# Decays by running products, and fewer raw weights held, in a fused retention and two-expert kernel

## Chip, cores, metric

The kernel runs on one core of a Trainium2 chip. The metric is the device time of one launch, in microseconds (us), as the median of several runs. Engines: TensorE (PE in the profile, its weight loads PEld), VectorE (DVE), ScalarE (ACT), GpSimd (POOL), and SyncE (SP), whose queue issues nearly all DMAs.

## What is computed

A retention layer (linear attention with a decay for each head) over two sequences of 768 positions, 8 heads of 64, in blocks of 64; then two experts, 512 to 2048 to 512 (squared ReLU) and 512 to 1536 to 512 (sigmoid gate), on the 1536 rows.

```python
# for each block of 64 positions
intra = (q_b @ k_b.T) * Dmask            # Dmask[i, j] = lam ** (i - j) for i >= j, else 0
out_b = intra @ v_b + (q_b * lam ** (i + 1)) @ state
state = lam ** 64 * state + (k_b * lam ** (63 - i)).T @ v_b
...
x = retention output as (1536, 512)
g = relu(x @ w_in) ** 2
x = g @ w_out
x = (sigmoid(x @ w_gate) * (x @ w_val)) @ moe2_w_out
```

## The kernel before, in words

Data are float32. A product of float32 matrices is made as three products of rounded halves (hi, lo): a hi part is a cast on ScalarE (`whi`, `xh`, `gh`, `ah`, `xch`), a lo part a subtraction on VectorE (`wlo`, `xl`, `gl`, `al`, `xcl`).

The weights come as raw words of 8 bytes. `load_w` brings one raw tile of 512 KB into a buffer of the pool `wp`, `scale_words` turns it with two ScalarE operations (lines 153 and 158) into two halves, and `join_words` puts these together with a shift and an add on VectorE (lines 164 and 169). Two weights go together as a couple: `couple_act`, `couple_dve`, `couple_split` are the ScalarE part, the VectorE part and the hi and lo split. Each whole weight is also stored to DRAM (`w32`) for later stages, 4 us of planner time after its add. Weights of the second expert are converted one at a time (`conv_act`, `conv_dve`) in the stage after the first Strassen stage.

The order on each engine is the order of the program text; a planner clock (`clock`, moved by `passed`, matmuls at 0.2267 us) only places the entries of an agenda (`at(pos, fn)`), such as splits of x, loads and stores. Nothing in the program text waits by hand: an operation waits for its operands and for the earlier users of the buffer that it gets. The pool `wp` has 27 buffers of 4 KB per partition, shared by q/k and k/v tiles, raw weights, couples, the split blocks of x and the weights of the Strassen stages; `up` has 27 of half that size.

Stages in time:

1. The lead: decays (`powers`, `decay_rows`, `decay_table`), loads, attention of the first two pairs of chunks (`PAIRS`, `LEAD`), with filler matmuls between (`warm_up`). Decays are powers: POOL computes W = lam ** ex; ScalarE's queue stores it to `w_dram`; SP loads the table D from there with a shifted row for each partition; 16 products on PE spread W into the rows L. For a pair: `att_scores`, `att_mask` (scores times D), `keys_of` and `query` (decayed k and q, on GpSimd), `att_uv`, `state_a` and `state_b` (states), `att_out`, `settle`, `att_past`, `att_x` (output split into x0).
2. A loop of 16 steps (`step_1`) for the first expert on the first 512 rows: 12 matmuls of `stage_a` (line 576) and 12 of `stage_b` of the step before (line 590), with the attention of the other four pairs between them (`SLOTS`, `LOADS`). `combine_x` splits the sums of the other rows' x blocks during the last steps.
3. `strassen` for the first expert's input product on the other 1024 rows: 8 units of 7 blocks of 6 matmuls (line 790), in the order B11, T4 of the unit before, T1, T2, B22, T3, B21. Weights of the next unit are split meanwhile (`load_a`, `combine_a`, `high_a`, `low_a`).
4. `pair_out` (line 1181), the first expert's output product, with the conversion of the second expert's weights.
5. The same for the second expert (`step_2`, `strassen` with 12 units, `blocks_out`).

## Time and profile before

| | |
|---|---|
| median of 3 runs | 626.39 us (625.79 to 628.44) |
| the profiled execution | 627.19 us |
| its span, first to last instruction | 625.3 us |
| PE busy | 584.6 us (93%) |
| VectorE / ScalarE / GpSimd busy | 452.3 / 340.5 / 59.9 us |
| mean granted TensorE clock | 0.984 of full speed |

Times in rows are from the start of the span. Busy PE includes matmuls in flight, so a stage's matmul count says more than its busy share.

### The profile page before, as it was taken

How to read it: one execution, taken by the hardware profiler on the slowest of the kernel's cores; microseconds unless marked ns; L12 is line 12 of the kernel's file. 1: busy time of each engine (PE TensorE's matmuls, PEld its weight loads, DVE VectorE, ACT ScalarE, POOL GpSimd, SP SyncE). 2: the span in 40 equal slices, each digit the busy share in tenths (PEclk: the TensorE clock that was granted, in tenths of full speed). 3: DMA queues.
4: the chain of work that ended last, by engine and by line, in shares of the span. 5: the costliest groups of instructions: out<-in, count | busy, mean ns of one | idle time of the engine just before them, and what ended most of it. 6: DMA issues, size and time to landing. Idle time of an engine off the chain costs nothing.

```text
span 625.3 us, 10317 instructions
## 1 busy us (share of the span) xinstructions
PE 584.6 (93%) x3924; PEld 471.7 (75%) x3924; DVE 452.3 (72%) x640; ACT 340.5 (54%) x538; POOL 59.9 (10%) x54
## 2 busy tenths in 40 slices
PE   7679998997888789999999999999999999999997
PEld 6657877865666667788888888888887888878885
DVE  2559978679657666766774688787477886779975
ACT  2267664597533453767664766454445634476561
POOL 4341354000000000000000000011011011000000
PEclk9869999998989999999999999999999999999999
DMA  8957995673214432999999699988544878397581
GB/s 304 396 212 281 332 305 187 220 246 134 68 68 124 163 116 88 304 368 415 412 409 380 226 338 286 349 281 248 133 116 102 239 213 210 133 363 291 180 329 67
DMA packets 69475, 150.63 MB, mean 241 GB/s; under 512 B 7089, under 2 KB 15281, under 8 KB 69426
## 3 DMA queue, kind: packets, MB, share of 16 engines
q1 hardware_dynamic: 65184, 144.08, 64.7%
q0 software_dynamic: 3360, 3.93, 4.2%
q10 hardware_dynamic: 882, 1.97, 1.0%
q8 instruction: 30, 0.49, 0.3%
q14 instruction: 19, 0.16, 0.1%
HBM read 106.17 MB, written 42.21 MB: 237 GB/s over the span
## 4 chain that ended last, share of the span: by engine, by line
PE 71%; DVE 11%; ACT 8%; DMA 5%; issue 4%; SPq 0%; DVEq 0%; ACTq 0%
PE p L790 20%; PE p L576 15%; PE p L1181 14%; PE p L590 10%; PE p L1110 7%; DMA qk<-in_qk 3%; PE p L477 2%; DVE c L804 2%; DVE al L769 2%; DMA gr<-gs 2%; ACT ah L763 2%; DVE wlo L228 1%; ACT s L799 1%; ACT whi L225 1%; DVE gq L977 1%
## 5 line engine op out<-in xcount | busy, mean ns | idle before, releaser
L790 PE MATMUL p<-xch,ah 128*128 128x512 f32 x280 | 112.2, 401 | 14.6 <-DVE c L804 10.3
L790 PE MATMUL p<-xch,al 128*128 128x512 f32 x280 | 109.9, 392 | 0.0
L790 PE MATMUL p<-xcl,ah 128*128 128x512 f32 x280 | 109.6, 391 | 0.0
L790 PEld LDWEIGHTS p<-xch,ah 128*128 128x128 f32 x280 | 52.9, 189 | 34.2 <-DVE c L804 13.6
L790 PEld LDWEIGHTS p<-xch,al 128*128 128x128 f32 x280 | 52.9, 189 | 11.4
L790 PEld LDWEIGHTS p<-xcl,ah 128*128 128x128 f32 x280 | 53.0, 189 | 10.4
L1110 PE MATMUL p<-gq,wq 128*128 128x512 f32 x252 | 57.9, 390 | 1.0 <-DVE wq L1067 1.0
L799 ACT COPY s<-p 128x512 f32<-128x512 f32 x60 | 34.8, 587 | 40.5 <-PE p L790 40.3
L1110 PEld LDWEIGHTS p<-gq,wq 128*128 128x128 f32 x252 | 47.1, 188 | 11.7 <-DVE wq L1067 1.6
L169 DVE CUSTOM_DVE_ANT_0 j<-j,r 128x1024 uint16<-128x1024 uint16 (+1 forms) x52 | 47.8, 920 | 4.5 <-ACT r L158 0.5
L153 ACT ACTIVATE j<-raw 128x512 f32<-128x512 f32 x68 | 45.5, 669 | 8.3 <-DMA raw<-in_w 6.7
L1181 PE MATMUL p<-g2l,whi 128*128 128x512 f32 x128 | 49.8, 389 | 0.0
L1181 PE MATMUL p<-g2h,wlo 128*128 128x512 f32 x128 | 49.8, 389 | 0.0
L1181 PE MATMUL p<-g2h,whi 128*128 128x512 f32 x128 | 49.8, 389 | 0.0
L804 DVE TENSOR_TENSOR c<-p,s 128x512 f32<-128x512 f32 x60 | 40.5, 685 | 12.4 <-PE p L790 12.4
L576 PE MATMUL p<-xh,whi 128*128 128x512 f32 x160 | 45.1, 405 | 1.2 <-ACT xh L539 1.2
L158 ACT ACTIVATE r<-raw 128x512 int32<-128x512 uint32 x68 | 45.2, 665 | 1.4 <-PE p L576 1.4
L625 ACT CAST gh<-g 128x512 fp32r<-128x512 f32 x28 | 17.4, 620 | 49.3 <-DVE g L617 25.5
L576 PE MATMUL p<-xh,wlo 128*128 128x512 f32 x160 | 43.7, 395 | 0.0
L576 PE MATMUL p<-xl,whi 128*128 128x512 f32 x160 | 43.6, 395 | 0.0
L738 POOL DMA_DIRECT2D as<-w x6 | 5.6, 933 | 382.7 <-DMA as<-w 355.8
L627 DVE TENSOR_TENSOR gl<-g,gh 128x512 fp32r<-128x512 f32 x28 | 21.0, 748 | 26.7 <-ACT gh L625 26.7
(140 smaller groups left out, 1087.8 us busy)
## 6 DMA issues: line engine op xcount, KB each, us to landing
raw<-in_w SPq DMA_DIRECT2D x68, 512.0 KB, 7.1
w<-j SPq DMA_DIRECT2D x68, 256.0 KB, 4.9
u<-w SPq DMA_DIRECT2D x52, 256.0 KB, 5.1
a<-w SPq DMA_DIRECT2D x20, 512.0 KB, 4.1
g<-g SPq DMA_DIRECT2D x32, 256.0 KB, 4.2
g<-g SPq DMA_DIRECT2D x16, 512.0 KB, 8.0
kv<-in_kv SPq DMA_DIRECT2D x12, 512.0 KB, 7.6
gr<-gs SPq DMA_DIRECT2D x24, 256.0 KB, 5.7
```

The lines of the kernel that those rows point to most:

```text
L153: nc.scalar.activation(j, t[:, :, 1].bitcast(F32), AF.Prelu, scale=2.0**-80 if flip else 2.0**-112, alpha=2.0**-32 if flip else 2.0**32,)
L158: nc.scalar.activation(r, low, AF.Copy, scale=2.0**-29)
L169: nc.vector.tensor_tensor(out=j, in0=j, in1=r, op=ALU.add)
L576: nc.tensor.matmul(acc, lhsT=a[:, kk * P : (kk + 1) * P], rhs=b[:, kk, :], start=i == 0, stop=i == 11,)
L590: nc.tensor.matmul(acc[e], lhsT=a[:, e * P : (e + 1) * P], rhs=b, start=first and i == 0, stop=last and i == 2,)
L625: nc.scalar.copy(gh, src)
L627: lambda: nc.vector.tensor_tensor(out=gl, in0=src, in1=gh, op=ALU.subtract)
L790: nc.tensor.matmul(acc, lhsT=w[:, col, kk * P : (kk + 1) * P], rhs=x[:, kk, :], start=start and i == 0, stop=stop and i == 5, skip_group_c ...
L799: nc.scalar.copy(s, acc)
L804: nc.vector.tensor_tensor(out=c, in0=acc, in1=s, op=ALU.add)
L1110: nc.tensor.matmul(acc[k], lhsT=a[:, wn], rhs=block_of(b, gn), start=first and n == 0, stop=last and n == 3 * len(group) - 1,)
L1181: nc.tensor.matmul(acc[e, t], lhsT=a[:, e * P : (e + 1) * P], rhs=b[:, t, :], start=first and i == 0, stop=last and i == 2,)
```

## The change

Decays become running products. A table of steps (lam, with 0 at the head of each row) and a table of spots (1 where a product starts) are made, and two scans on VectorE multiply along: one gives D, one gives the rows L; W is lam times the last column of D. The power, the stores to `w_dram`, the loads of D and the 16 products on PE are gone. All lead loads but q6 go through SP in one line. The order of the lead is another: the first pair is masked at once and put out before the second pair's scores; the first two weights are converted one by one and not as a couple; the fillers are 40, 12, 30 and 8 matmuls; `settle` is on ScalarE for the two lead pairs; v2 and v8 are loaded later. `couple_act` loads only weights of the first expert, and three raw weights of the second are loaded 14 us of planner time before `pair_out`. In `step_1`, `couple_act` stands at the end. The square in odd steps is on ScalarE as in even ones. Stores of whole weights come 7 us after their add and not 4. B21 is split last but two, and the places of the x sums are shifted.

```diff
-FILL = (16, 24, 44)
+FILL = (40, 12, 30, 8)
...
-    couples = [((1, 0, 0), (1, 1, 0))]
+    couples = [((1, 0, 0),), ((1, 1, 0),)]
...
-            at(clock[0] + 4.0, stored)
+            at(clock[0] + 7.0, stored)
...
         if more:
-            load_w(2)
+            load_w(sum(key[0] == 1 for key in to_load[: len(keys)]))
...
+        shift = unit("shift", I32)
+        nc.gpsimd.iota(shift, pattern=[[0, H], [1, SUB]], base=0, channel_multiplier=1)
...
+        nc.vector.memset(by_seq(step_d)[:, :, :, 0:1], 0.0)
+        nc.scalar.copy(seen, warm[:, 0:1])
...
         nc.vector.tensor_scalar(
+            out=spot_d, in0=shift, scalar1=float(2 * SUB - 1), scalar2=None, op0=ALU.is_equal
         )
...
         nc.vector.scalar_tensor_tensor(
+            out=spot_d, in0=shift, scalar=float(SUB - 1), in1=spot_d,
+            op0=ALU.is_equal, op1=ALU.add,
         )
...
+        nc.vector.memset(by_seq(step_l)[:, :, :, 0:1], 0.0)
+        nc.vector.memset(spot_l, 0.0)
+        nc.vector.memset(by_seq(spot_l)[:, :, :, 0:1], 1.0)
+        lam_r = pairs_of(lam8)
+        nc.vector.tensor_copy(by_seq(step_d)[:, :, :, 1:], lam_r.to_broadcast([P, 2, 4, SUB - 1]))
+        nc.gpsimd.tensor_copy(lam_half[half(0)], lam_r[half(0)])
+        for s in range(2):
+            nc.gpsimd.tensor_copy(lam_half[half(1), s], lam_r[half(1), 1 - s])
+        nc.gpsimd.tensor_copy(by_seq(step_l)[:, :, :, 1:], lam_half.to_broadcast([P, 2, 4, SUB - 1]))
+
+        def scan(out, step, spot):
+            nc.vector.tensor_tensor_scan(
+                out=out, data0=step, data1=spot, initial=0.0, op0=ALU.mult, op1=ALU.add
+            )
+
+        scan(flat(D), step_d, spot_d)
+        nc.vector.tensor_tensor(
+            out=pairs_of(W), in0=lam_r, in1=decay[:, :, :, SUB - 1 :], op=ALU.mult
         )
+        scan(flat(rows), step_l, spot_l)
+        nc.vector.tensor_tensor(out=G, in0=lam_half, in1=L[:, :, :, SUB - 1 :], op=ALU.mult)
...
-        nc.vector.tensor_copy(seen, o_t[pair][1][:, 1, 3, SUB - 1 :])
+        copy = nc.scalar.copy if pair[0] < LEAD else nc.vector.tensor_copy
+        copy(seen, o_t[pair][1][:, 1, 3, SUB - 1 :])
...
-        if ph == 1 and f % 2:
-            nc.scalar.activation(r, acc[0], AF.Relu)
-            nc.vector.scalar_tensor_tensor(
-                out=g, in0=acc[0], scalar=0.0, in1=r, op0=ALU.max, op1=ALU.mult
-            )
-        elif ph == 1:
+        if ph == 1:
...
-            lambda: split_x("B21", b21),
...
             lambda: split_x("T3", t["T3"]),
+            lambda: split_x("B21", b21),
...
         attend(2 * f)()
-        couple_act()
...
         last()
+        couple_act()
...
-        powers()
-        load("q0 q7 v0 v6 w v1")
-        decay_table()
-        load("q1 q8", nc.scalar)
-        load("v7 w w w")
+        load("q6", nc.scalar)
+        decays()
+        load("q0 q7 v0 v6 w q1 q8 v1 v7 w w w q2 q9")
         warm_up(WARM)
...
-        decay_rows()
...
-        keys_of(0)
-        keys_of(6, nc.vector)
-        query(6)
-        query(0)
-        query(7)
         att_scores(first)
         warm_up(FILL[0])
+        keys_of(0)
+        query(0)
+        query(6)
+        run(att_mask(first))
+        keys_of(6, nc.vector)
         att_uv(first)
         warm_up(FILL[1])
+        query(7)
+        couple_act()
         state_a(first)
-        state_b(first)
         keys_of(1)
+        mid = decayed(st_t[first][1])
         query(1)
+        att_out(first)
+        settle(first)
+        run(couple_dve())
+        plus(S[2], uv_t.pop(first)[1], mid)
+        att_scores(second)
+        att_past(first)
+        warm_up(FILL[2])
+        tt[0] = decayed(S[2], nc.gpsimd)
         keys_of(7)
         query(8)
-        att_scores(second)
-        warm_up(FILL[2])
-        run(att_mask(first) + att_mask(second))
+        run(att_mask(second))
+        x = att_x(first)
+        lo = couple_split()
+        run(x)
+        run(lo)
         couple_act()
-        load("q2 q9")
-        att_out(first)
-        settle(first)
         att_uv(second)
-        att_past(first)
-        x = att_x(first)
+        state_a(second)
+        load("v2 v8")
+        att_out(second)
+        settle(second)
+        warm_up(FILL[3])
+        att_past(second)
+        x = att_x(second)
         run(couple_dve())
         run(x)
         lo = couple_split()
-        state_a(second)
-        att_out(second)
-        settle(second)
-        att_past(second)
-        x = att_x(second)
-        run(lo + x)
+        run(lo)
         couple_act()
         state_b(second)
...
-        combine_x(1, [T1 + d for d in (-25, -23, -21, -18.5, -16, -13, -10.5, -7, -4, 1, 4)])
+        combine_x(1, [T1 + d for d in (-25, -22, -19.5, -17, -14, -10, -7, -4, -1, 2, 4)])
...
+        for k in range(3):
+            at(T2 - 14.0 + k, lambda: load_w(1))
```

## Rows read from the trace of the kernel before

**Rows 1.** Busy time by stage: stretch, length, each engine's busy us (instructions), PEclk, DMA share, GB/s.

```profile
0.00:37.39 37.39, 24.41 (x641) 22.18 (x641) 13.68 (x24) 8.38 (x14) 11.76 (x16) 0.90 0.93 351
37.39:50.20 12.81, 11.77 (x40) 8.59 (x43) 9.80 (x11) 10.06 (x17) 7.37 (x5) 0.77 0.27 88
50.20:122.28 72.08, 70.12 (x1196) 56.21 (x1196) 61.03 (x63) 42.22 (x68) 22.55 (x15) 1.00 0.81 282
122.28:162.07 39.79, 34.29 (x136) 25.35 (x133) 31.94 (x36) 30.65 (x45) 0.00 (x0) 0.96 0.50 175
162.07:261.04 98.97, 85.38 (x350) 65.34 (x349) 63.54 (x100) 45.27 (x75) 0.00 (x0) 0.98 0.39 131
261.04:348.09 87.05, 87.05 (x385) 72.09 (x385) 57.87 (x86) 54.84 (x87) 0.00 (x0) 1.00 1.00 384
...
443.29:562.93 119.64, 118.62 (x518) 96.34 (x517) 89.91 (x135) 62.86 (x100) 12.01 (x12) 1.00 0.65 193
```

**Rows 2.** The chain that ended last, whole run: start us, us, what.

```profile
261.04 87.05 PE p L1181 x384
```

**Rows 3.** The same chain, up to 60 us.

```profile
6.92 11.26 DMA qk<-in_qk
...
30.86 0.85 PE p L477 x24
31.71 2.13 issue
...
37.39 5.50 PE p L576 x12
```

**Rows 4.** Timeline of the lead, GpSimd and VectorE: start us, us, instruction, idle before.

```profile
9.18 1.04 POOL L393 TENSOR_TENSOR kd<-kv,W 128x512 f32<-128x512 f32 x1 [3.80 <-DMA kv<-in_kv]
...
17.68 1.27 POOL L386 TENSOR_TENSOR qd<-qk,rows 128x512 f32<-128x512 f32 x1
...
18.68 4.09 DVE L403 TENSOR_TENSOR at<-p,D 128x512 f32<-128x512 f32 x4 [3.96 <-DMA D<-w_dram]
```

**Rows 5.** Waits from 160 to 261 us: us in total, times, longest.

```profile
DVE al L769 <- PE p L790: 28.6, 7, 6.9
...
PE p L790 <- DVE c L804: 9.9, 7, 2.4
```

**Rows 6.** The chain from 162 to 262 us.

```profile
179.19 8.47 PE p L790 x29
...
196.40 2.83 PE p L790 x11
```

**Rows 7.** Instructions on raw weights, up to 160 us: duration ns min/median/max, first and last start.

```profile
L141 SPq DMA_DIRECT2D raw<-in_w x36: 328/428/887, 3.3 to 142.2; - x36
L153 ACT ACTIVATE j<-raw x32: 652/667/706, 13.3 to 142.9; 128x512 f32<-128x512 f32 x32
```

**Rows 8.** Timeline of GpSimd and VectorE, 82 to 97 us.

```profile
83.33 3.97 POOL L386 TENSOR_TENSOR qd<-qk,rows 128x512 f32<-128x512 f32 x2
...
86.18 2.20 DVE L169 CUSTOM_DVE_ANT_0 j<-j,r 128x2048 uint16<-128x2048 uint16 x1
...
95.68 0.69 DVE L164 TENSOR_SCALAR j<-j 128x1024 int32<-128x1024 int32 x1
96.40 1.23 DVE L169 CUSTOM_DVE_ANT_0 j<-j,r 128x2048 uint16<-128x2048 uint16 x1
```

**Rows 9.** Groups on ScalarE, 122 to 162 us: busy us, mean ns, idle before.

```profile
L225 ACT CAST whi<-j 128x1024 fp32r<-128x1024 f32 x5 | 5.2, 1044 | 1.6 <-DVE j L169 1.5
...
L613 ACT ACTIVATE g<-r 128x512 f32<-128x512 f32 x3 | 1.9, 633 | 0.1
```

**Rows 10.** Waits from 122 to 162 us.

```profile
PE p L590 <- ACT whi L225: 4.7, 4, 3.0
ACT gh L625 <- DVE g L608: 3.5, 2, 2.7
```

**Rows 11.** Raw weights, 250 to 350 us.

```profile
DMA to landing us min/median/max: 5.0/7.5/8.5
```

## Prediction

> **What bounds the kernel now.** I first cut the profiled span at the borders of its stages and read TensorE's row in each [rows 1]. From 261 to 348 us the first expert's paired half has PE busy for all 87.05 us, so 384 matmuls in 87.05 us give the price of a 512-column matmul when nothing is late: 0.2267 us [rows 2]. Every other stage is then its matmuls times 0.2267 plus what it loses. The second Strassen stage (443 to 563) has 516 of them, 117.0 us of work in 119.64: it loses 2.7 us over 12 units. The first one (162 to 261) has 8 x 42 + 12 = 348, 78.9 us of work, and takes 98.97: it loses 20.1 us, with the same code. The last six steps of the loop before it (122 to 162) hold eleven blocks of 12 matmuls, 29.9 us, in 39.79: 9.9 lost. The middle of that loop (50 to 122) has PE idle for 2.0 us in 72, so little can come from there. The lead takes 37.39 us before the first expert matmul, and the next three blocks (8.16 us of work) take 12.81, at a granted clock of 0.77. What can be had lies in three places, the lead with its first blocks, the last steps and the first Strassen stage, and I went to each with the chain of waits.

> In the lead the chain hangs on a load of q, 11.26 us from issue to landing [rows 3], and the decay table D, which goes through DRAM, lands later still: the four masks start at 18.68, after VectorE has idled 3.96 us for D [rows 4]. [...]

> In the first Strassen stage the longest wait of VectorE is not for data: the low halves of the next unit's weights (`al`) wait seven times for TensorE, 28.6 us in all, and TensorE then waits seven times for the totals `c` behind them, 9.9 us [rows 5]. The chain says which matmul: 29 or 11 of them before `al` starts, that is five sixths into the last block but one of the unit, T3 [rows 6]. T3's fifth matmul is the last reader of the high half of the current unit's sums. `al` doesn't read that tile; it takes its buffer. The count agrees. The pool wp has 27. When `al` of the next unit is written, seven split x blocks (14), the current unit's four tiles, the next unit's a, its sums, its two high halves (4), the a after it (1) and the raw weights are alive. 36 raw loads were issued by 160 us and 32 were converted [rows 7]: 4 raw tiles wait for the stage after. 14 + 4 + 4 + 1 + 4 = 27, and `al` is the 28th.

> **The change, part by part.**

> *Fewer raw weights held.* `couple_act` now loads only weights of the first expert, so none of the four lies in wp during this stage; three are loaded 14 us (in the planner's clock) before its end, when no further `a` is fetched. `al` finds a free buffer and starts when its inputs are there. What is late next? Per unit VectorE has some 8 us of work and TensorE 9.52; ScalarE less. The yardstick is the second Strassen stage, where 12 units lose 2.7 us [rows 1]: 0.22 a unit, 1.8 for eight. I add 2.8 for the start, where four evacuations and the last splits stand ahead of the snapshots on ScalarE. 78.9 + 1.8 + 2.8 = 83.5: a gain of 15.5. Bounds: 18 (no more than the yardstick's loss) and 3.5, if another wait takes over and only some of the 9.9 comes back.

> *Decays on VectorE, loads in one line.* The power, two stores to DRAM, the two loads of D from there and 16 small products on PE go. In come a 512-wide iota, some ten fills and copies, and two scans of 512 elements. The trace has no scan; the nearest rows are VectorE's operations of that size or larger, 0.69 to 1.23 us alone and up to 2.20 beside GpSimd [rows 8]. I take 1.23 a scan. Even two at 2.20 and a copy of 0.69 ahead of them are 5.1 us behind lam, SP's first load, while `keys_of(0)` waits for v until 9.18 anyway [rows 4]: they cost nothing. Their cover is v0 and q7; without it they would cost their 3 to 5 us. What it buys: the first masks need only the scores, and SP no longer stands at the load of D, so that v7 and three weights follow at once. Queue order is now q0 q7 v0 v6 w q1 q8 v1 v7, w w w, q2 q9. The lead moved 351 GB/s at a DMA share of 0.93 [rows 1]: 377 at full share, 1.39 us per 512 KB. From v0 at 9.18, v1 is five loads later: 16.1, v7 17.5. GpSimd then has five pieces in a row: keys 1, query 1, the decayed state, keys 7, query 8, three of 1.04 and two of 1.27 [rows 4]: 21.8. From there the old trace gives the rest: 0.85 us for the part of the output that needs the state, and 37.39 - 31.71 - 2.13 = 3.55 from that to the first expert matmul [rows 3]. 26.2. The two stalls without a releaser come somewhere in an engine program of much the same length; filler and waits can hide them, so 0 to 4.3: I take 1.3, a third. First expert matmul at 27.5, 9.9 earlier. Bounds 26.2 and 31.

> *The first blocks.* The fillers (40, 12, 30, 8 in place of 16, 24, 44) stand elsewhere: the last stretch has 8. At full clock the three blocks are 8.16 us. I leave 1.4 us for the first use of a couple of two weights, whose cast alone is 1.04 [rows 9] with a subtraction behind it: 9.6, a gain of 3.2. Bounds 0 (the lower clock level as now) and 4.65. Together with the lead 13, from 6.4 to 15.8.

> *Odd steps by two ScalarE operations.* VectorE loses 0.69 us per odd step, ScalarE gains a Square of 0.63 [rows 9]. In the last six steps the cast `gh` waited 3.5 us for that product, twice, because VectorE was busy with sums of weights [rows 10]; two Squares are 1.3. +2.2. Moving the split of B21 (1.05 on ScalarE) 22 us back takes one cast out of the crowd ahead of the casts `whi` for which TensorE waits 4.7 us there [rows 10]: +1.3. Sum 3.5; bounds -1.3 (the Squares, with no wait saved) and 9.9.

> *`couple_act` at the end of a step.* On ScalarE it stands between the same neighbours as now, but what it converts is needed by VectorE at once and not a step later. Cover: in the middle PE takes 72.08 us for 17 blocks [rows 1], 8.5 us for a step of two, against 5.6 for the ring of casts below. Zero, with a rival. The stores come 3 us later on SP, which only frees loads behind them. *Settle on ScalarE* in the lead: a copy of one column, zero.

> *The stage after.* 24 conversions follow each other every 3.46 us ((87.05 - 4) / 24); with three raw tiles in flight instead of four a load has 10.4 us. They landed in at most 8.5 [rows 11]. Zero.

> Sum: 13 + 3.5 + 15.5 = 32. The profiled execution took 627.19 us, of which 625.3 are its span; 627.19 - 32 = 595.2. It was 0.8 above the median 626.39, so 594.4 for the median. Differences under 0.5% (3 us) this measurement can't tell from none.

> **Rivals.**

> The buffers don't do it: the freed slot given to `al` has a late reader too, or TensorE then waits as long for ScalarE's snapshots. For it: which of several free buffers is given I can't see. Against: 27 is met exactly. Gain there 3.5 instead of 15.5: 606.4. Chance 0.13.

> The lead gains half. GpSimd's five pieces lie beside VectorE's masks, states and subtractions. Two queries took 3.97 us where one takes 1.27, and VectorE's add 2.20 instead of 1.23, when both worked [rows 4, 8]. [...] Chance 0.12. [...]

> A ring in the loop: cast `whi` (1.04), four conversions (0.667 each), shift (0.69), add (1.23), next `whi` [rows 7 to 9]: 5.6 us. It decides where it is longer than a step. In the last six steps a step is 5.44 us, and VectorE, busy for 31.94 of 39.79 us [rows 1], also makes the sums and splits of x there, each about as long as the add. With two of them ahead of the shift the ring is 8.0: 48 us for six steps, 8 lost and not 3.5 gained: 606. Against: those splits fit beside ScalarE's conversions. Chance 0.08.

> All goes to its better bound: 15.8 + 6 + 18: 586.6. Chance 0.09.

> Slower: conversions starve in the stage from 261 on. With three in flight their interval is the larger of 3.46 and a third of the landing time. DMA is at a share of 1.00 there [rows 1], so landing may stretch. It costs nothing up to 10.4 us; at 14.4 all 32 us are gone (24 x 1.34); at 15, 631. The slowest of before took 8.5. Chance 0.05.

> Neither lead nor buffers move anything: 622 to 627. Chance 0.03.

> **How the numbers follow.** The forecast has 0.50 (own range 588 to 600). The range 585 to 608 takes in it and the rivals at 586.6, 601, 606 and 606.4, and leaves out the last two and the ends of the others. Faster 0.92, the same 0.03, slower 0.05.

> **What would show it.** After the change `al` no longer waits for TensorE in the first Strassen stage, which takes 82 to 86 us. The first expert matmul starts at 26 to 30 us, and the masks of the first pair run before 11. `gh` no longer waits for VectorE's product in odd steps; the last six steps take 35 to 37 us. The stages from then on keep their lengths. Wrong would make it: `al` or `c` waiting as before; ScalarE waiting for raw weights in the paired half; the lower clock level past 30 us; or VectorE's shift waiting for ScalarE in every step.

## The result and the profile after

The changed kernel takes 598.61 us (median of 4 runs, 596.02 to 599.45) where the kernel before took 626.09 beside it: a ratio of 0.955, with an interval of 0.9509 to 0.9591. On another chip it had 0.9508 [0.9482, 0.9534]. The profiled execution took 596.02 us, with a span of 594.3 against 625.3 before. Busy time by stage, in the columns of [rows 1]:

```profile
0.00:34.66 34.66, 24.26 (x615) 22.36 (x615) 15.18 (x28) 7.36 (x15) 12.64 (x18) 0.89 0.95 366
34.66:46.81 12.15, 10.40 (x40) 7.58 (x42) 10.74 (x11) 9.52 (x16) 8.35 (x5) 0.88 0.49 172
46.81:116.05 69.24, 69.24 (x1197) 55.73 (x1197) 55.49 (x59) 47.01 (x75) 26.10 (x15) 1.00 0.83 294
116.05:149.12 33.07, 31.70 (x136) 24.44 (x133) 28.55 (x32) 32.46 (x49) 0.00 (x0) 1.00 0.38 136
149.12:229.13 80.01, 79.78 (x350) 65.26 (x349) 64.40 (x100) 45.90 (x74) 0.00 (x0) 1.00 0.52 178
229.13:316.17 87.04, 87.04 (x385) 72.13 (x385) 57.70 (x86) 55.57 (x87) 0.00 (x0) 1.00 0.98 384
```

Set against [rows 1], the lead gives 2.7 us (13 were forecast for it and the first blocks together), the first blocks 0.7, the middle of the loop 2.8 (forecast 0), the last steps 6.7 (3.5) and the first Strassen stage 19.0 (15.5): 31.9. The paired half is as long as it was, and the stages behind it lose 0.9 between them, which leaves the 31.0 by which the span shrank. These are two single executions, and the one of after was the fastest of its four; the medians are 27.5 apart. The total came out near the forecast; its split did not.

The chain of the whole run answers to [rows 2] and [rows 6]: 312 of the Strassen stage's matmuls now stand in one piece, with nothing between them.

```profile
157.68 71.45 PE p L774 x312
```

That is 0.229 us a matmul, the price of the paired half (0.2267) and 1% more. The longest wait of [rows 5], `al` for TensorE, is no longer among VectorE's waits (150 to 240 us). What heads them is short and costs TensorE nothing: `c` waits for the matmuls that it adds up, at most 0.8 us at a time.

```profile
DVE c L788 <- PE p L774: 8.5, 14, 0.8
DVE g L868 <- ACT r L867: 4.3, 6, 1.9
```

The raw weights, in the manner of [rows 7]: 32 loads and 32 conversions by 149 us, all of the first expert, so no raw tile is held.

```profile
L141 SPq DMA_DIRECT2D raw<-in_w x32: 327/361/939, 3.3 to 116.2; - x32
L153 ACT ACTIVATE j<-raw x32: 637/667/700, 11.4 to 139.8; 128x512 f32<-128x512 f32 x32
```

In the stage behind (216 to 320 us; [rows 11] for before) a load still lands in less than the 10.4 us that three tiles allow. ScalarE waits there six times for a raw weight, 2.5 us in all, and the stage is not longer for it.

```profile
DMA to landing us min/median/max: 5.6/7.6/8.9
```

VectorE and GpSimd in the lead, from two timelines (start us, us, instruction, idle before), beside [rows 4]: a scan of 512 elements takes the 1.23 us that was assumed, the first two masks run at 8.36 and not at 18.68, and GpSimd's five pieces end at 22.2 (forecast 21.8).

```profile
4.05 1.23 DVE L300 TENSOR_TENSOR_SCAN D<-step_d,spot_d 128x512 f32<-128x512 f32 x1
...
8.36 1.29 DVE L391 TENSOR_TENSOR at<-p,D 128x512 f32<-128x512 f32 x2 [0.85 <-PE p L354]
...
16.72 1.04 POOL L381 TENSOR_TENSOR kd<-kv,W 128x512 f32<-128x512 f32 x1 [3.51 <-DMA kv<-in_kv]
...
20.93 1.28 POOL L374 TENSOR_TENSOR qd<-qk,rows 128x512 f32<-128x512 f32 x1
```

And yet the first expert matmul starts at 34.66, not 27.5. The chain of the lead, for [rows 3]:

```profile
12.69 1.59 issue
14.28 0.27 PE p L315 x2
14.55 1.78 PE p L465 x79
16.34 0.76 PE p L354 x44
17.09 3.42 issue
20.52 0.80 PE p L354 x18
21.33 0.09 PE p L354
21.42 1.14 PE p L465 x15
22.56 3.32 PE p L315 x30
25.88 1.75 PE p L408 x64
27.62 1.83 PE p L465 x94
29.45 0.55 PE p L315 x8
30.00 0.67 PE p L465 x20
30.67 2.32 issue
32.99 0.52 PE p L465 x9
...
33.53 1.08 ACT xh L528 x2
...
34.66 4.37 PE p L565 x12
```

Three stalls without a releaser, 7.33 us, where the prediction took 1.3. They have a pattern. From 14.28 to 17.09 the pieces add up to 125 matmuls, with some records missing. From 20.52 to 27.62 they add up to 18 + 1 + 15 + 30 + 64 = 128; there is no stall behind these. In windows ahead of the three resumptions (10 to 12, 16 to 18, 29 to 31 us) and ahead of 27.62 (23 to 25) the trace's instruction queue q8 has one packet of 0.02 MB each. In the whole run it has 30 packets and 0.49 MB, 16 KB a packet, for TensorE's 3898 recorded matmuls and as many weight loads, some 130 of each for a packet:

```profile
q8 instruction: 1, 0.02, 3.4%
...
q8 instruction: 30, 0.49, 0.3%
```

So TensorE's program comes in blocks of 128 matmuls with their weight loads, and PE stands where the next one has not landed. That is a reading; the experiments test it.

The last steps, for [rows 10] (waits from 116 to 149 us): `gh` no longer waits for a product of VectorE, and TensorE's waits for `whi` fall from 4.7 us to 0.6.

```profile
PE p L579 <- DVE wlo L231: 0.8, 3, 0.3
PE p L579 <- ACT whi L228: 0.6, 1, 0.6
```

### The profile page after: what moved, and what is told of

It is laid out like the page before. It is cut to its first block, busy times and chain, and to the rows that moved or that the text cites. A ratio compares the mean times of both kernels' runs of the same rounds, so it can differ in the third digit from the quotient of the medians.

```text
span 594.3 us, 10287 instructions
## 1 busy us (share of the span) xinstructions
PE 574.1 (97%) x3898; PEld 469.5 (79%) x3898; DVE 446.5 (75%) x637; ACT 347.0 (58%) x548; POOL 65.2 (11%) x56
## 4 chain that ended last, share of the span: by engine, by line
PE 74%; ACT 9%; DVE 6%; DMA 5%; issue 4%; SPq 1%; DVEq 0%; ACTq 0%
PE p L774 26%; PE p L565 16%; PE p L1165 15%; PE p L579 10%; DMA gr<-gs 4%; PE p L465 3%; PE p L1094 1%; DVE gq L961 1%; DMA kv<-in_kv 1%; PE p L408 1%; ACT xch L657 1%; ACT ah L747 1%; PE p L354 1%; DVE c L788 1%; DVE wq L1051 1%
## 5 line engine op out<-in xcount | busy, mean ns | idle before, releaser
L774 PE MATMUL p<-xch,ah 128*128 128x512 f32 x280 | 110.1, 393 | 1.2 <-ACT s L783 0.8
L774 PEld LDWEIGHTS p<-xch,ah 128*128 128x128 f32 x280 | 52.6, 188 | 15.5 <-ACT s L783 3.9
L1094 PEld LDWEIGHTS p<-gq,wq 128*128 128x128 f32 x252 | 47.1, 188 | 12.3 <-DVE wq L1051 1.7
L788 DVE TENSOR_TENSOR c<-p,s 128x512 f32<-128x512 f32 x60 | 41.3, 688 | 20.6 <-PE p L774 20.5
L565 PEld LDWEIGHTS p<-xh,whi 128*128 128x128 f32 x160 | 29.8, 191 | 7.6 <-ACT xh L528 1.3
```

Source lines behind the costliest of these rows:

```text
L565: nc.tensor.matmul(acc, lhsT=a[:, kk * P : (kk + 1) * P], rhs=b[:, kk, :], start=i == 0, stop=i == 11,)
L774: nc.tensor.matmul(acc, lhsT=w[:, col, kk * P : (kk + 1) * P], rhs=x[:, kk, :], start=start and i == 0, stop=stop and i == 5, skip_group_c ...
L788: nc.vector.tensor_tensor(out=c, in0=acc, in1=s, op=ALU.add)
L1094: nc.tensor.matmul(acc[k], lhsT=a[:, wn], rhs=block_of(b, gn), start=first and n == 0, stop=last and n == 3 * len(group) - 1,)
```

## The experiments

All are edits of the changed kernel, except where the one before is named. Times are medians; each ratio is to the kernel before on the same chip. The hold runs and before_fewer_raws ran on one chip; wide_fill, no_fill, no_raw and dve_square on a second; early_blocks, b21_second, couple_early and after_again on a third. Only the last four have after beside them (after_again); elsewhere a difference to its 598.61 us is one between two measurements, and the ratios are the safer comparison.

### The raw weights held in the Strassen stage

**hold4, hold3, hold2.** Four, three or two raw weights of the second expert are loaded in the loop again, and so many fewer late (n is 4, 3 or 2; with 4 and 3 none is left to load late).

```diff
+HELD = ((2, 0, 0), (2, 0, 1), (2, 0, 2), (2, 1, 0))[:n]
-            load_w(sum(key[0] == 1 for key in to_load[: len(keys)]))
+            load_w(sum(key[0] == 1 or key in HELD for key in to_load[: len(keys)]))
...
-        for k in range(3):
+        for k in range(3 - n):
```

> The changed kernel with four raw weights of the second expert loaded during the loop again, so that four lie in the pool wp through the first Strassen stage. Buffer theory (the gain of that stage is the buffer that al no longer waits for): al waits for TensorE again, seven times and over 20 us in all, the stage is back at 94 to 99 us from 80.0, and the time goes from 598.6 to 613 to 618. Rival (the stage gained because ScalarE comes out of the loop less late): the stage stays at 80 to 84, the time within 3 us of 598.6.

> The same with three raw weights held. Buffer theory: 14 + 4 + 4 + 1 + 3 = 26, so the first al of a unit gets the last free buffer and only the second al waits, up to the last matmul of T3: the stage takes 88 to 96 us, the time is 606 to 615. A theory of traffic (the raw loads themselves, or the later conversions) would make the loss grow evenly with the number held: three quarters of that with four.

> The same with two raw weights held. Buffer theory: both al find a free buffer, al waits for TensorE under 2 us in all, the stage is 80 to 82 us and the time within 2 us of 598.6. Theory of traffic: half of the loss with four, some 8 us.

Measured: hold4 615.86 us (0.9838 [0.9792, 0.9884]), hold3 600.57 (0.9581 [0.955, 0.9613]), hold2 596.85 (0.9523 [0.9505, 0.9541]). With four the wait is back (waits of hold4, 150 to 240 us), seven times and about as long as the 28.6 us of [rows 5]:

```profile
DVE al L754 <- PE p L775: 26.3, 7, 5.1
```

With three it is gone, and the chain has the 312 matmuls in one piece again, 71.49 us from 160.84 on.

So three held tiles fit, and the fourth is what `al` waits for: the border lies where the count of 27 put it for the first `al` of a unit. The count did not hold for the second `al`: with three held it would be the 28th, and it does not wait, so my expectation for hold3 was wrong. A reading that no run tests: the first `al` is the last to read the next unit's `a`, and the second comes behind it, when that buffer can be free. Hold3 is still 3.7 us slower than hold2, with the intervals apart; its 312 matmuls take as long but begin at 160.84 and not at 158.32, and why is open.

**before_fewer_raws.** The kernel before with this one part of the change: `load_w` in `couple_act` takes weights of the first expert only, three come late.

```diff
-            load_w(2)
+            load_w(sum(key[0] == 1 for key in to_load[: len(keys)]))
...
+        for k in range(3):
+            at(T2 - 14.0 + k, lambda: load_w(1))
```

> The kernel before with nothing but the raw weights of the second expert loaded late, as in the change. Buffer theory: the first Strassen stage falls from 99.0 to 80 to 85 us and the time from 626.1 to 606 to 612; lead and loop stay as they were. Rival (the rest of the change made the stage faster): under 4 us faster.

Measured: 609.56 us, 0.9734 [0.9706, 0.9763], and the 312 matmuls in one piece (71.50 us). One edit of a load's place is worth 17.1 us (626.62 - 609.56) on its own; hold4 takes 17.3 away (615.86 against 598.61, measured apart; on its own chip 15.3 against hold3 and 19.0 against hold2). Put in or taken out, it is more than half of the change.

### The lead

**wide_fill and no_fill.** The fillers as a quarter of the matmuls with 512 columns each, or none between the steps of the lead.

```diff
-WARM = 44
-FILL = (40, 12, 30, 8)
+WARM = 11
+FILL = (10, 3, 8, 2)
...
-            nc.tensor.matmul(t[:, 0:P], lhsT=warm, rhs=warm, start=True, stop=True)
+            nc.tensor.matmul(t, lhsT=warm[:, 0:P], rhs=warm, start=True, stop=True)
```

```diff
-FILL = (40, 12, 30, 8)
+FILL = (0, 0, 0, 0)
```

> The changed kernel with the lead's fillers four times as wide and a quarter as many (512 columns; 11, 10, 3, 8, 2 in place of 44, 40, 12, 30, 8): the same PE time for 100 fewer matmuls. Code theory (the stalls called issue come when TensorE has run through a block of its program, every 128 matmuls, and the next 16 KB block of instructions lands no faster than one per 6.2 us under these loads): one of the three stalls (1.59, 3.42, 2.32) goes or is covered by the wait for keys 7, the first expert matmul comes at 28 to 31 us and not 34.7, and the time falls by 3 to 6 us. Rival (the stalls stand at fixed times, for a load or another queue): they stay near 12.7, 17 and 31, and the time stays within 1.5 us.

> The changed kernel without the four later fillers (90 matmuls fewer; the first 44 stay). [...] Rival: stalls at the same times, first expert matmul near 34 less 3.3 for the filler of 30, and the clock lower.

Measured: wide_fill 594.74 us (0.9485 [0.9434, 0.9535]), first expert matmul at 33.34 (28 to 31 was expected); no_fill 593.11 (0.9439 [0.941, 0.9468]), at 31.24. The interval of no_fill lies below both that after has, at 0.955 and at 0.9508; that of wide_fill overlaps both, so its gain in time is not shown. In wide_fill two stalls are left of three, 2.10 and 3.78 us, ending at 16.58 and 29.18. The timeline of TensorE in no_fill:

```profile
15.00 0.70 PE L465 MATMUL p<-at,kv 64*64 64x64 f32 x14 [1.14 <-issue]
...
21.26 1.01 PE L408 MATMUL p<-kv,kd 64*64 64x64 f32 x44 [1.65 <-issue]
...
27.55 0.27 PE L465 MATMUL p<-qd,S 64*64 64x64 f32 x1
```

The first two stalls are within a microsecond of their old times, which alone would fit the rival too. But they stand before other work and at the same count: 222 and 349 recorded matmuls lie ahead of them in no_fill as in after, and 477 ahead of the third, which is the border at 27.62 in after. They end at 15.00, 21.26 and 27.55: 6.26 and 6.29 us apart. In after 14.28 and 20.52 are 6.24 apart, and 20.52 and 32.99 twice 6.24, with the border at 27.62 between them. The run b21_second below, whose lead is that of after, shows what happens there: its PE comes to that border earlier and stalls, and its four stalls end at 14.29, 20.52, 26.69 and 32.88, 6.2 us apart each time.

```profile
26.16 0.52 issue
...
29.83 3.06 issue
```

So in this stretch a block lands some 6.2 us behind the one before it, whatever PE computes in between. In no_fill and early_blocks PE entered each block as it landed, so these can't tell landing from entry; in after the block entered at 27.62 was followed 5.37 us later, at 32.99, so there the time does not count from the entry. Without fillers the lead has the lower clock level for longer (from 14 to 18 us the granted clock is 0.50, in after 1.00), and is still shorter: the fillers bought a clock in a stretch that waited for its program.

**no_raw.** Seven of the raw weights are not loaded in the lead; their conversions read the first raw tile. This leaves out loads, and the expert's weights are other ones.

```diff
             ph, f, u = key = to_load.pop(0)
+            if raw_t.get("first") is not None and clock[0] < 8.0 and not looped:
+                raw_t[key] = raw_t["first"]
+                continue
...
+            raw_t.setdefault("first", t)
```

> The changed kernel with seven raw weights not loaded in the lead (the first raw tile is read in their place, so the weights of the first steps are wrong). It takes 3.7 MB off the loads of the lead. If instruction blocks land late because they share the DMA engines with a full queue, the stall at 31 us (2.32) shrinks below 0.8 and that at 17 (3.42) below 2.5, the first expert matmul coming 2 to 5 us earlier. If a block takes 6 us whatever the load, all three stalls stay as long.

Measured: 593.35 us (a single execution). The first two stalls are as in after (1.25 and 3.42 us; the second was expected to shrink), with the DMA share still at 0.98 to 1.04 from 12 to 20 us. The third is gone. From 28 us on, ahead of its place and on it, the DMA engines now have next to nothing to do (windows of no_raw; columns as in [rows 1]):

```profile
28.00:30.00 2.00, 2.00 (x73) 1.83 (x67) 1.24 (x3) 0.16 (x1) 0.00 (x0) 1.00 0.09 35
30.00:32.00 2.00, 0.83 (x31) 0.69 (x28) 0.65 (x2) 1.26 (x3) 0.00 (x0) 1.00 0.03 8
```

The DMA share there is 0.09 and 0.03, against 1.01 and 1.05 in after, and `xh` starts at 30.74, 2.8 us earlier. The packet of the block in question is at 27.8 us on the instruction queue, 3.7 behind the one before it; in after it is at 30.6, 6.2 behind. So a block was late while the DMA engines were full of q, k, v and weights, and in time when they were not; this rests on one execution.

**early_blocks.** No fillers between the steps, and 94 of 64x64 at the start instead of 44 of 128x128: the first block is left earlier, and the packets behind it should come earlier.

```diff
-WARM = 44
-FILL = (40, 12, 30, 8)
+WARM = 94
+FILL = (0, 0, 0, 0)
...
-            nc.tensor.matmul(t[:, 0:P], lhsT=warm, rhs=warm, start=True, stop=True)
+            nc.tensor.matmul(t[0:64, 0:64], lhsT=warm[:, 0:64], rhs=warm[:, 0:64], start=True, stop=True)
```

> After without the fillers between the steps of the lead, and with 94 fillers of 64x64 at its very start instead of 44 of 128x128, so that the first 128-matmul block of TensorE's program is left at about 6 us and not at 8. Theory (a next block lands some 6.2 us after the last border was crossed): blocks land near 12.3, 18.5 and 24.7 us, the stall before the last past matmuls ends 2 to 3 us earlier than the 27.55 without fillers, and the first expert matmul begins at 28.5 to 30 us: 591 to 592.5 us, ratio 0.939 to 0.943. Rival (the stalls are set by when the data and the other engines arrive, the blocks only happen to lie there): the first expert matmul stays at 31 us and the time at 593, as without fillers. Second rival: the fillers themselves delay the first scores, and the time is that of after.

Measured: 591.27 us, 0.9426 [0.9405, 0.9446]. The last two stalls end where the theory put them, 18.61 and 24.86 (expected 18.5 and 24.7), 6.25 apart:

```profile
18.61 0.46 PE L354 MATMUL p<-qk 64*64 64x64 f32 x16 [1.31 <-issue]
...
24.86 1.22 PE L465 MATMUL p<-at,kv 64*64 64x64 f32 x33 [2.60 <-issue]
```

The packets on q8 come earlier too: here in the windows 8 to 9, 16 to 17 and 22 to 23 us, in no_fill in 12 to 14, 18 to 20 and 24 to 25. The first rival falls as to the stalls. But only 0.8 us of the 2.7 by which the last stall ends earlier than in no_fill reach the first expert matmul, which starts at 30.44 and not by 30 as expected: with 50 more fillers ahead, 97 matmuls of the attention and not 47 are left behind that border, and they run at the lower level: 65 take 2.50 us, 38 ns each, where 94 take 1.83 us in after (mean granted clock of the lead 0.77 against 0.89). 50 of them at 38 ns make up the 1.9 us that are missing. Against after on the same chip (after_again) 5.3 us are gained and the intervals are apart; against no_fill, on another chip, the intervals overlap. Its median is the lowest of this study.

### The last steps

**dve_square.** The odd steps' square as a product on VectorE again.

```diff
+        if ph == 1 and f % 2:
+            nc.scalar.activation(r, acc[0], AF.Relu)
+            nc.vector.scalar_tensor_tensor(
+                out=g, in0=acc[0], scalar=0.0, in1=r, op0=ALU.max, op1=ALU.mult
+            )
-        if ph == 1:
+        elif ph == 1:
```

> The changed kernel with the squares of the odd steps on VectorE again. My sum gave this part 2.2 us of the last six steps: the stretch from the ninth stage_b to the first Strassen block goes from 33.1 to 35 to 36, the cast gh waits 3 us and more for VectorE's product, and the time is 1 to 4 us longer. Rival (ScalarE is the bound there, and a Square less helps it): the time is the same or 1 to 2 us shorter.

**b21_second.** The split of B21 second again, with the old places.

```diff
             lambda: split_x("B11", b11),
+            lambda: split_x("B21", b21),
...
-            lambda: split_x("B21", b21),
...
-        combine_x(1, [T1 + d for d in (-25, -22, -19.5, -17, -14, -10, -7, -4, -1, 2, 4)])
+        combine_x(1, [T1 + d for d in (-25, -23, -21, -18.5, -16, -13, -10.5, -7, -4, 1, 4)])
```

> After with the split of B21 second in the list of the combinations again, and the eleven places of before. Theory (the move of B21 takes one split off the chain on VectorE and ScalarE in the last expert steps): the last steps are 34 to 37 us long instead of 33.1, the time is 600 to 602 us, ratio 0.957 to 0.961. Rival (the squares on ScalarE and the conversions made the last steps shorter, the order does nothing): the last steps stay at 33 us and the time at that of after within 0.3%.

**couple_early.** `couple_act` at its old place in a step.

```diff
         attend(2 * f)()
+        couple_act()
         if prev:
             stage_b(*prev.pop())
...
         last()
-        couple_act()
```

> After with couple_act called at its old place in step_1, ahead of the previous step's second matmuls, and not at the end of the step. Prediction's step (moving it costs and gains nothing): time within 0.3% of after, the stretch of the steps in the middle 69 to 70 us long, as in after. Rival (moved to the end it closes a ring of waits with the shift and the add, and so costs time): 2 to 8 us faster than after, in the steps in the middle. Second rival (the late place is what made the steps in the middle 2.8 us shorter than before): 2 to 3 us slower than after, and those in the middle 71.5 to 72.5 us long.

Measured: dve_square 601.6 us (0.9581 [0.9544, 0.9617]), b21_second 601.4 (0.9577 [0.955, 0.9604]), couple_early 600.48 (0.957 [0.9551, 0.9588]). The last steps of each, from the windows of the three traces:

```profile
118.99:156.00 37.01, 32.30 (x137) 24.28 (x133) 30.25 (x34) 30.17 (x45) 0.00 (x0) 1.00 0.34 122
```

```profile
117.46:154.30 36.84, 33.50 (x137) 25.40 (x133) 30.03 (x33) 33.89 (x50) 0.00 (x0) 0.95 0.34 122
```

```profile
48.21:118.64 70.43, 69.67 (x1197) 55.96 (x1197) 55.12 (x58) 44.33 (x71) 24.98 (x15) 1.00 0.81 281
118.64:153.40 34.76, 32.37 (x136) 24.18 (x133) 28.73 (x32) 33.61 (x50) 0.00 (x0) 1.00 0.41 146
```

In after they take 33.07. So the Squares on ScalarE are worth 3.9 us there, the place of B21 3.8, and the late `couple_act` 1.7; the first two were forecast at 2.2 and 1.3, the third at zero. Against after_again on their chip, b21_second is 4.8 us slower and couple_early 3.9, with the intervals apart. For dve_square there is no after beside it; its interval overlaps that of the first measurement of after, and its profiled execution, 604.59 us, was its slowest; its 3.9 rests on that one stretch and on the waits below. The three add up to 9.4, and together they gave 6.7. That each removes waits of the same chain (`gh`, `whi`), so that the last one to come finds less, fits the waits; no run undid two at once. In the middle `couple_act` is worth 1.1 more (70.43 against 69.3); the other two change nothing there. The ring that the prediction feared does not show: the old place is slower, not faster. With the Square on VectorE the wait of [rows 10] is back and longer (waits of dve_square):

```profile
ACT gh L614 <- DVE g L597: 5.6, 2, 3.0
PE p L579 <- ACT whi L228: 3.9, 3, 1.9
```

**after_again.** The changed kernel beside early_blocks, b21_second and couple_early.

> The changed kernel itself, beside the three others on one chip: both theories expect the ratio that it had, 0.955 within 0.004, the same three stalls before the first expert matmul (1.6, 3.4 and 2.3 us, give or take half a microsecond) and a first expert matmul at 34.7 us.

Measured: 596.56 us, 0.9508 [0.9482, 0.9534]; first expert matmul at 34.76. The first blocks took 13.3 us there and 12.15 in after, so differences of a microsecond in that stretch mean nothing. Middle and last steps were 69.3 and 33.1, as in after; those lengths carry the readings above.

## Why the prediction came out

594.4 us were forecast, with 585 to 608, and 598.61 came. The mechanism that carried most of it, the buffer, was right; the lead failed. That the sum came so close is luck: in the two profiled executions the lead and the first blocks gave 9.6 less than forecast, and the middle, the last steps and the first Strassen stage 9.5 more.

**The first Strassen stage.** The step "27 is met, and `al` is the 28th" is shown from both sides, with the border between the third and the fourth held tile; the count went wrong only for the second `al`. Its size was low: 83.5 us forecast, 80.01 measured. The allowance of 4.6 us for losses (1.8 by the yardstick of the second Strassen stage and 2.8 for the start) should have been 1.1. The rival that the buffers don't do it is refuted by before_fewer_raws.

**The lead.** This is the step that failed. GpSimd's five pieces ended at 22.2 as reckoned, so "from there the old trace gives the rest", 0.85 + 3.55, and "the two stalls without a releaser ... I take 1.3". From 22.2 to 34.66 there were 12.5 us in place of 5.7. Three stalls of 7.33 in all took the place of 1.3. The first two stood ahead of and within the second scores, so these came at 20.5 and the filler of 30 behind them (3.32 us, at a granted clock of 0.50 from 22 to 26 us) stood on the path until 25.88; the third stood there itself. I had treated the stalls as a loss that lies somewhere; in these runs they follow a schedule of their own, one block in 6.2 us, and work that comes earlier meets it sooner. In before, whose lead stood for loads and D first, the chain met it twice, 4.25 us (the stalls end at 27.64 and 33.84, 6.20 apart); the third of it that I took was an estimate, and no run shows it. The rival that the lead gains half was nearer to it in amount, but its cause, GpSimd and VectorE in each other's way, was not: the five pieces took 1.04 to 1.28 each. One GpSimd instruction did take longer beside VectorE, elsewhere and at no cost. Of GpSimd's two equal copies of four columns the first starts at 4.10, behind the start of the first scan (4.05 to 5.28), and takes 1.155 us, to within 0.03 us of the scan's end; the second takes 0.187, and a copy of eight columns ahead of the scan 0.438. Both scans take the same 1.23 us. GpSimd's busy time up to 8 us, 3.10 us in after, is 3.10 or 3.11 in after_again, no_fill, dve_square, early_blocks, b21_second and couple_early.

```profile
L296 POOL COPY lam_half<-lam x2: 187/671/1155, 4.1 to 5.2; 64x4 f32<-64x4 f32 x2
L294 POOL COPY lam_half<-lam x1: 438/438/438, 3.6 to 3.6; 64x8 f32<-64x8 f32 x1
```

So the copy that started behind the scan took until it ended; why, no run shows. The fill (5.45) needs the copies and the second scan (6.08) the fill; the two scans and the fill took 3.3 us in a row, still ahead of v0, whose keys start at 9.00.

**The first blocks.** 9.6 forecast, 12.15 measured. The first twelve matmuls took 4.37 us and not 2.72, after a third stall that left PE idle, so one of the signs of being wrong came: the lower clock level past 30 us (granted clock 0.50 from 34.66 to 36). The clock is not the whole of it. In no_raw, without that stall, the granted clock is 1.00 there and the first twelve take 2.9 us, but the stretch still takes 12.3 (31.86 to 44.19). The term for the first use of a couple, 1.4 us, was too small: `wlo` alone took 2.33 us, and TensorE stood 1.48 for it in after and 1.16 in no_raw. The bound "0 (the lower clock level as now)" was the nearer one.

**The last steps.** The two mechanisms named were the right ones, and were under-sized (3.5 against 6.7). I valued the Squares by the waits of `gh` alone and the split by its own length on ScalarE; taken away they cost 3.9 and 3.8. In dve_square the cast that comes later is followed by longer waits for `whi` (3.9 us against 0.6), which the sum had left out.

**The middle, and `couple_act`.** "Zero" was wrong: 2.8 us were gained there. PE's idle time fell from 1.96 us, which the prediction had set aside as too little, to nothing, and its busy time from 70.12 to 69.24. The late place of `couple_act` is 1.1 of the 2.8. Of the other 1.7 the cause stays open; no run took the later stores or the order of loads by themselves.

**Behind.** The conversions in the paired half did not starve: 87.04 us, and 8.9 us at most for a load.

**A slip in the range.** The rival "all goes to its better bound" counted 6 us for the last steps, whose bound in the text is 9.9. With 9.9 it would have come to 582.7 us, outside the range that was meant to hold it.

## What to carry to other kernels

Count the tiles of a pool that are alive at the instruction that waits: here a fourth raw tile, loaded a stage before it is used, cost 15 to 19 us, and the wait named neither the load nor the pool. A stall of TensorE without a releaser, in a stretch with full DMA queues, is to be held against the count of its instructions since the last such stall before it is given a price; there filler instructions are not free, they bring the next border nearer (without them the first expert matmul came 3.4 us earlier). Gains of several edits in one stretch need not add up: undo them one at a time.

## What the runs showed of the hardware

A scan over 512 fp32 elements on 128 partitions took 1.23 us on VectorE. A GpSimd copy of 64x4 that came just behind its start took 1.155 us, to within 0.03 us of the scan's end, and the same copy behind it 0.187 (after).
